# A Strassen-type first GEMM in the second feed-forward layer: seven block products for eight, in five of six token chunks

## The chip, the cores and the metric

The kernel runs on one core of a Trainium2 chip. The metric is the device time of one execution in microseconds (us): the median of 3 runs before the change is 853.1 us (852.42 to 856.21). TensorE (PE) multiplies; each of its matmuls has a weight load of its own (PEld), which the trace records apart. VectorE (DVE), ScalarE (ACT) and GpSimd (POOL) do the element-wise work, SyncE (SP) issues the DMAs.

## What is computed

An mLSTM-like attention over 4 batches x 768 positions, and then two feed-forward layers on its 3072 rows of 320 numbers:

```
x = np.ascontiguousarray(attn_out.transpose(0, 2, 1, 3)).reshape(B * S, H * D)   # (3072, 320)
h = x @ w_in;  g = np.maximum(0.01 * h, h);  x = (g @ w_out)                      # layer 0: 320 -> 2048 -> 320
h = np.maximum(x @ w_in, 0.0);  return (h * h @ w_out).astype(np.float32)         # layer 1: 320 -> 2048 -> 320
```

All in float32. The change is in layer 1, in the product `x @ w_in`.

## The kernel before

Tokens go in 6 chunks of 512 (128 positions of each of the 4 batches), the hidden width of 2048 in 16 tiles of 128 (index j). Full precision comes from splitting each number into a rounded part H and a rest L (both float32r) and adding three products: wH xH + wL xH + wH xL. One tile j of a chunk in layer 1 is:

- `moe_h` (L462 to 486): the contraction over 320 is two blocks of 128 and a rest of 64. Eight matmuls of 512 columns go into one PSUM bank `hp` (L472): three for each of the two blocks, and two for the rest, whose H and L parts lie stacked in one 128-row tile. Then ACT takes the ReLU out of the bank into `g` (L483), DVE squares it (L484), ACT rounds it into `gH` (L485), DVE subtracts into `gL` (L486).
- `out2` (L540 to 563): for each batch three matmuls of 320 columns (L552 to 554) add this tile's share of the second GEMM into one of four banks; after j = 15 the banks are copied out by ACT or DVE (L560, L562) and sent to memory (L563). The four banks rotate over six.

Layer 1's weights arrive during the last chunk of layer 0 and the first of layer 1, and are unpacked by DVE (L432, L434, L437, L448, L443) and ACT (L436, L439), 16 tiles one after the other. `x2_split` (L528) splits a chunk's layer-1 input.

The order of the work on each engine is not written by hand. Every operation is entered with an engine, an estimated length and a key; `Sched.order` (L96) simulates the whole program with these lengths, turns the result round to get new keys (`backward`), repeats that 6 times and then tries 160 random shifts of the keys, and keeps the best plan. Each engine then executes its list strictly in that order. A PSUM bank or an SBUF buffer under a tag is given to its next user when all readers of the last one are done.

Of the kernel before, what the change touches and what calls it, by code (L numbers as in the profile page):

```python
# [8 lines left out]
F32 = mybir.dt.float32  # L9
# [5 lines left out]
ALU = mybir.AluOpType  # L15
# [37 lines left out]
class Sched:  # L53
    SAME = {"PE": 0, "DVE": 130, "ACT": 120, "POOL": 100, "SP": 0}

    def __init__(self):
        self.nodes, self.slots, self.idle = [], {}, []

# [70 lines left out]
    def backward(self, plan, total):  # L129
# [23 lines left out]
    def forward(self):  # L153
# [26 lines left out]
        while done < len(self.nodes):  # L180
# [78 lines left out]
            else:  # L259
# [5 lines left out]
                for m in n.outs:  # L265
                    m.ndep -= 1
                    if m.ndep == 0:
                        t = max(d.end + (self.SAME[m.eng] if d.eng == m.eng else 100) for d in m.deps)
                        heapq.heappush(at, (max(t, now, m.after), 1, m.seq))
# [7 lines left out]
def act(n, psum=False):  # L277
    return (n + (61 if psum else 112)) / 1.2
# [11 lines left out]
def mlstm_moe_kernel(  # L290
# [122 lines left out]
    def weight(layer, j, key):  # L413
# [24 lines left out]
        f32 = lambda: ft().bitcast(F32)  # L438
        op("ACT", act(WR), key, lambda: A.copy(w.t[:, 0:WR], f32()), r=[(fb, fr)], w=[(w, "H"), (w, "C")])  # L439
        c0 = 512 if layer == 0 else 576  # L440
# [22 lines left out]
    def moe_h(layer, c, lo, n, j, key, xk):  # L463
# [9 lines left out]

        op("PE", 8 * mm(n), key, pe, r=[(w, "H"), (w, "L"), (w, "C")] + [(x, k) for k in xk for x in (xH, xL)], w=[(hp, 0)])
        gH, gL = sb("gH", [128, BLK], F32R, 3), sb("gL", [128, BLK], F32R, 3)
# [61 lines left out]

    pools6 = ["attS", "atty", "attm", "acc0", "acc1", "acc2"]

    def out2(c, j, key):  # L540
        w = wt[1, j]
        gH, gL = gs.pop((1, c, 0, j))
        if j == 0:
            acc[1] = [ps(pools6[(4 * c + i) % 6]) for i in range(4)]
        first, last = j == 0, j == NF - 1
        for b in range(B):
            a = acc[1][b]

# [6 lines left out]

            op("PE", 3 * mm(DM), key, pe, r=[(w, "H"), (w, "L"), (gH, 0), (gL, 0)], w=[(a, 0)])
            if last:
                o = sb("aw", [128, DM], slots=3)
                if b % 2 == 0:
# [260 lines left out]
    for layer in range(2):  # L820
        for c in range(NCH):
# [3 lines left out]
            if layer == 1:  # L825
                x2_split(c, base - 20)
            for j in range(NF):
                if layer == 0 and c == 0:
                    continue
                key = base + U * j  # L830
                moe_h(layer, c, 0, BLK, j, key, range(4) if layer == 0 else range(3))
                if layer == 0:
                    out1(c, 0, BLK, j, key + ORDER["outk"] * U)
                else:
                    out2(c, j, key + ORDER["outk"] * U)
            if layer == 0 and c == NCH - 1:
# [69 lines left out]
```

## Time and profile before

| | |
|---|---|
| median of 3 runs | 853.1 us (852.42 to 856.21) |
| the profiled execution, its own time | 856.46 us |
| its span, first to last instruction | 854.7 us |
| PE busy | 836.0 us, 98% of the span, 5161 matmuls recorded |
| DVE busy | 533.6 us (62%) |
| ACT busy | 470.1 us (55%) |
| POOL busy | 97.9 us (11%) |
| TensorE clock granted, mean | 0.991 |

Busy shares are means over stages with different limits: attention with layer 0 reaches to about 510 us, layer 1 fills the rest, 58 us a chunk. A matmul's recorded length includes its way through the array, and matmuls overlap; what one costs in a stream is the distance from its start to the next one's.

### The profile page before, as it was taken

How to read it: one execution, taken by the hardware profiler on the slowest of the kernel's cores; microseconds unless marked ns; L12 is line 12 of the kernel's file. 1: busy time of each engine (PE TensorE's matmuls, PEld its weight loads, DVE VectorE, ACT ScalarE, POOL GpSimd, SP SyncE). 2: the span in 40 equal slices, each digit the busy share in tenths (PEclk: the TensorE clock that was granted, in tenths of full speed). 3: DMA queues.
4: the chain of work that ended last, by engine and by line, in shares of the span. 5: the costliest groups of instructions: out<-in, count | busy, mean ns of one | idle time of the engine just before them, and what ended most of it. 6: DMA issues, size and time to landing. Idle time of an engine off the chain costs nothing.

```text
span 854.7 us, 13738 instructions
## 1 busy us (share of the span) xinstructions
PE 836.0 (98%) x5161; PEld 719.3 (84%) x5166; DVE 533.6 (62%) x974; ACT 470.1 (55%) x933; POOL 97.9 (11%) x134
## 2 busy tenths in 40 slices
PE   9889989999999999999999999999999999999998
PEld 6778878787878877888788889899999999999997
DVE  6799975767676676766657898453443533533433
ACT  8588657757766785676455675343433433433332
POOL 3354731103010210001000000000000000000000
PEclk9799999999999999999999999999999999999999
DMA  7396452435344353552312432000000000000000
GB/s 217 115 324 206 134 162 84 156 100 170 100 153 147 122 158 116 152 160 94 99 69 77 161 136 69 1 32 1 1 31 0 17 15 1 31 1 1 32 1 31
DMA packets 52211, 78.58 MB, mean 92 GB/s; under 512 B 4337, under 2 KB 40785, under 8 KB 52145
## 3 DMA queue, kind: packets, MB, share of 16 engines
q1 hardware_dynamic: 52144, 77.71, 28.5%
q8 instruction: 40, 0.66, 0.3%
q14 instruction: 27, 0.21, 0.1%
HBM read 54.26 MB, written 4.01 MB: 68 GB/s over the span
## 4 chain that ended last, share of the span: by engine, by line
PE 74%; DVE 12%; SPq 4%; ACT 4%; DMA 3%; issue 2%; POOL 0%; DVEq 0%; ACTq 0%; POOLq 0%
PE hp L472 33%; SPq L620 4%; PE acc L503 3%; PE acc L554 3%; PE acc L553 3%; PE acc L552 3%; PE acc L505 3%; PE acc L504 3%; DMA aw<-Adram 2%; PE attS L678 2%; PE acc L508 2%; PE acc L509 2%; ACT aw L669 1%; PE atty L688 1%; DMA T<-X 1%
## 5 line engine op out<-in xcount | busy, mean ns | idle before, releaser
L472 PE MATMUL hp<-xH,w 128*128 128x512 f32 (+1 forms) x995 | 290.1, 388 | 4.9 <-DVE gL L480 3.6
L472 PEld LDWEIGHTS hp<-xH,w 128*128 128x128 f32 x995 | 178.2, 188 | 36.4 <-DVE gL L480 5.0
L472 PE MATMUL hp<-xL,w 128*128 128x512 f32 (+1 forms) x597 | 196.0, 383 | 0.0
L484 DVE TENSOR_TENSOR g<-g 128x512 f32<-128x512 f32 x96 | 66.3, 691 | 119.5 <-ACT g L483 119.5
L472 PEld LDWEIGHTS hp<-xL,w 128*128 128x128 f32 x597 | 111.2, 188 | 23.6
L483 ACT ACTIVATE g<-hp 128x512 f32<-128x512 f32 x96 | 57.3, 597 | 130.3 <-PE hp L472 130.2
L486 DVE TENSOR_TENSOR gL<-g,gH 128x512 fp32r<-128x512 f32 x96 | 66.3, 691 | 56.4 <-ACT gH L485 56.4
L485 ACT CAST gH<-g 128x512 fp32r<-128x512 f32 x96 | 59.6, 620 | 68.9 <-DVE g L484 68.9
L480 DVE TENSOR_TENSOR gL<-hp,gH 128x512 fp32r<-128x512 f32 (+1 forms) x103 | 66.9, 650 | 33.8 <-ACT hp L479 33.0
L478 ACT ACTIVATE gH<-hp 128x512 fp32r<-128x512 f32 (+1 forms) x103 | 58.1, 564 | 46.9 <-PE hp L472 41.8
L503 PE MATMUL acc<-gH,w 128*128 128x512 f32 (+1 forms) x206 | 82.2, 399 | 0.0
L505 PE MATMUL acc<-gL,w 128*128 128x512 f32 (+1 forms) x206 | 77.8, 378 | 0.6 <-DVE gL L480 0.6
L504 PE MATMUL acc<-gH,w 128*128 128x512 f32 (+1 forms) x206 | 77.6, 377 | 0.0
L554 PE MATMUL acc<-w,gL 128*128 128x320 f32 x192 | 59.3, 309 | 0.0
L553 PE MATMUL acc<-w,gH 128*128 128x320 f32 x192 | 59.3, 309 | 0.0
L552 PE MATMUL acc<-w,gH 128*128 128x320 f32 x192 | 59.2, 308 | 0.0
L479 ACT ACTIVATE hp<-hp 128x512 f32<-128x512 f32 (+1 forms) x103 | 57.6, 559 | 0.0
L672 POOL TENSOR_SCALAR_AFFINE_SELECT aw<-aw 128x512 f32<-128x512 f32 x48 | 32.2, 671 | 202.8 <-ACT aw L669 193.0
L669 ACT ACTIVATE aw<-aw,cs 128x128 f32<-128x128 f32 x160 | 50.6, 390 | 7.1 <-DMA aw<-Adram 6.8
L505 PEld LDWEIGHTS acc<-gL,w 128*128 128x128 f32 x206 | 38.7, 188 | 8.4 <-DVE gL L480 0.8
L503 PEld LDWEIGHTS acc<-gH,w 128*128 128x128 f32 x206 | 39.0, 189 | 5.8
L504 PEld LDWEIGHTS acc<-gH,w 128*128 128x128 f32 x206 | 38.9, 189 | 5.6
(165 smaller groups left out, 1447.8 us busy)
## 6 DMA issues: line engine op xcount, KB each, us to landing
T<-X SPq DMA_DIRECT2D x144, 120.0 KB
x<-in_wts_dram SPq DMA_DIRECT2D x16, 704.0 KB
aw<-Adram SPq DMA_DIRECT2D x40, 256.0 KB
nat<-in_nat_dram SPq DMA_DIRECT2D x24, 328.0 KB
qkr<-in_qk_dram SPq DMA_DIRECT2D x16, 360.0 KB
X<-in_wts_dram SPq DMA_DIRECT2D x8, 704.0 KB
T<-in_wts_dram SPq DMA_DIRECT2D x8, 704.0 KB
og<-in_og_dram SPq DMA_DIRECT2D x12, 320.0 KB
```

Source lines behind the costliest of these rows:

```text
L472: T.matmul(hp.t[:, 0:n], w.t[:, col:col + 128], x.t[:, kt, o], start=(s == 0), stop=(s == 7))
L480: op("DVE", dve(n), key, lambda: V.tensor_tensor(out=gL.t[:, 0:n], in0=h(), in1=gH.t[:, 0:n].bitcast(F32), op=ALU.subtract), r=[(hp, 0), ( ...
L484: op("DVE", dve(n), key, lambda: V.tensor_tensor(out=g.t, in0=g.t, in1=g.t, op=ALU.mult), r=[(g, 0)], w=[(g, 0)])
L485: op("ACT", act(n), key, lambda: A.copy(gH.t, g.t), r=[(g, 0)], w=[(gH, 0)])
L486: op("DVE", dve(n), key, lambda: V.tensor_tensor(out=gL.t, in0=g.t, in1=gH.t.bitcast(F32), op=ALU.subtract), r=[(g, 0), (gH, 0)], w=[(gL, 0)])
L503: T.matmul(a[t].t[:, o], w.t[:, hc:hc + 128], gH.t[:, 0:n], start=first, stop=False)
L504: T.matmul(a[t].t[:, o], w.t[:, lc:lc + 128], gH.t[:, 0:n], start=False, stop=False)
L505: T.matmul(a[t].t[:, o], w.t[:, hc:hc + 128], gL.t[:, 0:n], start=False, stop=last)
L552: T.matmul(a.t[:, 0:DM], gH.t[:, s], wH, start=first, stop=False)
L553: T.matmul(a.t[:, 0:DM], gH.t[:, s], wL, start=False, stop=False)
L554: T.matmul(a.t[:, 0:DM], gL.t[:, s], wH, start=False, stop=last)
L669: A.activation(aw.t[:, h], x[:, h], AF.Exp, bias=cs.t[:, 4 * g + h:4 * g + h + 1])
```

## The change

In chunks 1 to 5 of layer 1 two tiles j = 2p and 2p+1 become a pair, and the two 128-row blocks of the contraction times these two tiles are a 2 x 2 block matrix; the 512 tokens are cut into two halves of 256. The 2 x 2 by 2 x 2 block product is formed by Strassen's scheme in Winograd's form: seven block products instead of eight, each of three matmuls (H and L parts) of 256 columns. The rest of 64 rows stays as it was (two matmuls of 256 columns, four times a pair).

- `weight_sums` makes, once for each of the 8 pairs during chunk 0, the sums S1 to S4 of weight blocks on DVE and splits them (S4 in place of block A21, which is no longer needed). They lie in the buffers T, X, qkr, Cst, C32 of earlier stages.
- `x2_sums` replaces `x2_split` for chunks 1 to 5: sums T1 to T4 of the input's blocks, then the same splitting.
- `moe_pair` issues the products into two banks X and Y. Y collects a running sum; ACT copies it out of the bank four times between the products (256 columns each) into buffers `q`. At the end DVE adds q and the bank (L652), takes ReLU and square in one operation (L654), ACT rounds (L655), DVE subtracts (L656).
- `out2` gives its four products of a tile keys of their own (table `OUT`), so that the planner can put them between the block products; the two halves of odd tiles come out swapped and are read so. Its four banks are now fixed; the pairs use two `hp` banks and `acc1`, `acc2` in turn.
- Every product of a pair is entered as a write of its whole bank, so a copy from one half waits for, and holds up, products into the other. From layer 1 on, the planner counts 230 ns from PE to another engine, 250 ns back and 120 ns between the others, where it counted 100.

```
+COPY = 150
+OUT = (1, 2.5, 3, 5, 5.5, 7, 7.3, 7.6)
+    def edge(self, d, m):
+        return 100 if m.seq < self.late else 230 if d.eng == "PE" else 250 if m.eng == "PE" else 120
...
+    def weight_sums(p, key):
...
+        for i, w in enumerate((w0, w1)):
+            op("DVE", dve(256), key, lambda i=i, w=w: V.tensor_tensor(out=a.t[:, i], in0=w.t[:, 0:256].bitcast(F32), in1=w.t[:, 704:960].bitcast(F32), op=ALU.add),
...
+        for o, x, y, f, rd in ((S1, A21, A22, ALU.add, [(a, 1)]), (S2, S1, A11, ALU.subtract, [(s, 0), (a, 0)]),
+                               (S3, A11, A21, ALU.subtract, [(a, 0), (a, 1)]), (S4, A12, S2, ALU.subtract, [(a, 0), (s, 1)])):
...
+        op("ACT", act(3 * CH), key + 0.4, lambda: A.copy(sb_.t[:, at, 0], s3()), r=rd, w=[(sb_, (at, "H"))])
+        op("DVE", dve(3 * CH), key + 0.5, lambda: V.tensor_tensor(out=sb_.t[:, at, 1], in0=s3(), in1=sb_.t[:, at, 0].bitcast(F32), op=ALU.subtract),
...
+    def x2_sums(c, key):
...
+        for k, (o, a, b, rd) in enumerate(((T1, B12, B11, [(x, 0)]), (T2, B22, T1, [(x, 1), (t, 0)]), (T3, B22, B12, [(x, 0), (x, 1)]), (T4, B21, T2, [(x, 1), (t, 1)]))):
+            op("DVE", dve(256), key, lambda o=o, a=a, b=b: V.tensor_tensor(out=o(), in0=a(), in1=b(), op=ALU.subtract), r=rd, w=[(t, k)])
...
+    def moe_pair(c, p, key):
...
+        X, Y = [ps("hp") if p % 2 == 0 else ps(("acc1", "acc2")[i]) for i in range(2)]
...
+        def three(bank, half, a, b, start):
+            o = bank.t[:, 256 * half:256 * half + 256]
+            for i, (u, v) in enumerate(((a[0], b[0]), (a[1], b[0]), (a[0], b[1]))):
+                T.matmul(o, u(), v(), start=start and i == 0, stop=i == 2, skip_group_check=True)
+
+        def two(bank, half, i, w):
+            o = bank.t[:, 256 * half:256 * half + 256]
+            for k in range(2):
+                T.matmul(o, w.t[:, 576:704], xC.t[:, 2 + 2 * k + i], start=False, stop=k == 1, skip_group_check=True)
...
+        prod(Y, 0, A11, B11, 0, start=True)
+        copy(0, 256, 0, (q[0], 0, 0))
+        prod(X, 0, A12, B21, 0.5, start=True, tail=(w0, X, 0, 0))
+        prod(Y, 0, S2, T2, 2)
+        copy(0, 256, 2, (q[1], 1, 0))
+        prod(Y, 1, S3, T3, 3.5)
+        prod(Y, 0, S1, T1, 4)
+        copy(0, 256, 4, (q[1], 0, 1), (q[0], 1, 0))
+        prod(X, 1, S4, B22, 4.5, tail=(w0, X, 1, 1))
+        prod(Y, 1, A22, t4, 6, tail=(w1, Y, 1, 0))
+        op("PE", 2 * mm(256), key + 6.3 * U / 4, lambda: two(Y, 0, 1, w1), r=[(w1, "C"), (xC, 2), (xC, 4)], w=[(Y, 0)])
...
     def out2(c, j, key):
...
-            acc[1] = [ps(pools6[(4 * c + i) % 6]) for i in range(4)]
+            acc[1] = [ps(x) for x in pools4]
...
-            op("PE", 3 * mm(DM), key, pe, r=[(w, "H"), (w, "L"), (gH, 0), (gL, 0)], w=[(a, 0)])
+            op("PE", 3 * mm(DM), key + (OUT[4 * (j % 2) + b] * U / 4 if c else 0), pe, r=[(w, "H"), (w, "L"), (gH, h), (gL, h)], w=[(a, 0)])
...
+                elif j % 2 == 0:
+                    moe_pair(c, j // 2, key)
```

The order that the planner makes of it is the same on PE through all of attention and layer 0 and up to the second tile of layer 1's chunk 0, where the matmuls of one more tile are now drawn ahead of the second GEMM's products. DVE and ACT take the first operations of `x2_sums` and of `weight_sums` already during the last chunk of layer 0. Four places show what moved.

On PE, in the middle of a chunk of layer 1, before: one tile's eight matmuls into an `hp` bank (L472), then twelve for the second GEMM (L552 to 554; `w` is a weight tile, `gH` and `gL` the split hidden tile).

```order
L472 MATMUL hp_6861<-xH_6155,w7_5529 128x512 x4
L472 MATMUL hp_6861<-xL_6162,w7_5529 128x512 x2
L472 MATMUL hp_6861<-xH_6155,w7_5529 128x512
L472 MATMUL hp_6861<-xL_6162,w7_5529 128x512
L552 MATMUL attm_6725<-w5_5450,gH_6831 128x320
L553 MATMUL attm_6725<-w5_5450,gH_6831 128x320
L554 MATMUL attm_6725<-w5_5450,gL_6842 128x320
```

On PE in chunk 1 now, where pair 3 starts (Y is bank `acc2`, X is `acc1`; `X_6051` holds the weight sums S1 to S3 of this pair; L610 is a block product, L615 the rest of 64 rows, L673 to 675 the second GEMM):

```order
L610 MATMUL acc2_6546<-xH_5669,w6_5524 128x256 x2
L610 MATMUL acc2_6546<-xL_5673,w6_5524 128x256
L610 MATMUL acc1_6550<-xH_5669,w6_5524 128x256 x2
L610 MATMUL acc1_6550<-xL_5673,w6_5524 128x256
L615 MATMUL acc1_6550<-x2_0_5190,w6_5524 128x256 x2
L673 MATMUL attS_6438<-w4_5440,gH_6531 128x320
L674 MATMUL attS_6438<-w4_5440,gH_6531 128x320
L675 MATMUL attS_6438<-w4_5440,gL_6544 128x320
L610 MATMUL acc2_6546<-xH_5669,X_6051 128x256 x2
L610 MATMUL acc2_6546<-xL_5673,X_6051 128x256
```

Between the first product into Y and the second, for which Y must have been copied out, now stand the product into X, its rest and one group of the second GEMM.

On PE, still in chunk 1, now: the end of pair 4 in the `hp` banks (the rest into Y, `hp_6612`) and the beginning of pair 6 in the same two banks (`hp_6714` takes the bank that held X, `hp_6720` the one that held Y); before, the next use of a bank stood a whole tile later, as in the rows above.

```order
L673 MATMUL acc0_6456<-w7_5569,gH_6654 128x320
L674 MATMUL acc0_6456<-w7_5569,gH_6654 128x320
L675 MATMUL acc0_6456<-w7_5569,gL_6666 128x320
L615 MATMUL hp_6612<-x2_0_5190,w9_5642 128x256 x2
L610 MATMUL acc2_6650<-xH_5669,qkr_6127 128x256 x2
L610 MATMUL acc2_6650<-xL_5673,qkr_6127 128x256
L610 MATMUL hp_6714<-xH_5669,w12_5799 128x256 x2
L610 MATMUL hp_6714<-xL_5673,w12_5799 128x256
L610 MATMUL hp_6720<-xH_5669,w12_5799 128x256 x2
L610 MATMUL hp_6720<-xL_5673,w12_5799 128x256
```

Six matmuls of 256 columns stand between the last one into Y and the first into the same bank for the pair after next.

On DVE in chunk 0 of layer 1, from the eighth `gL` of that chunk to the tenth, before (the squaring is L484, `gL` is L486):

```order
L486 TENSOR_TENSOR gL_5954<-g_5932,gH_5952 128x512
L484 TENSOR_TENSOR g_5959<-g_5959 128x512
L486 TENSOR_TENSOR gL_5982<-g_5959,gH_5971 128x512
L484 TENSOR_TENSOR g_5987<-g_5987 128x512
L486 TENSOR_TENSOR gL_6010<-g_5987,gH_5999 128x512
```

and now, from the eighth to the ninth and on (squaring L490, `gL` L492, the sums of weight blocks L554 and L561, their lower parts L565 and L568):

```order
L492 TENSOR_TENSOR gL_6005<-g_5974,gH_5999 128x512
L565 TENSOR_TENSOR T_5924<-aw_5966,T_5924 128x384
L561 TENSOR_TENSOR aw_5966<-aw_5473,aw_5966 128x128
L490 TENSOR_TENSOR g_6010<-g_6010 128x512
L568 TENSOR_TENSOR w5_5483<-aw_5966,w5_5483 128x128
L554 TENSOR_TENSOR aw_6028<-w6_5524 128x256
L554 TENSOR_TENSOR aw_6028<-w7_5569 128x256
L492 TENSOR_TENSOR gL_6040<-g_6010,gH_6026 128x512
L561 TENSOR_TENSOR aw_6042<-aw_6028 128x128 x2
L561 TENSOR_TENSOR aw_6042<-aw_6042,aw_6028 128x128
```

Between two `gL` that stood one operation apart, five further ones of 128 to 384 columns now stand; the sums of all eight pairs lie so between the chunk's own operations.

## Rows read from the trace of the kernel before

**Rows 1.** Page of the profile: busy us, share of the span, instructions; granted clock in 40 slices.
```profile
PE 836.0 (98%) x5161; PEld 719.3 (84%) x5166; DVE 533.6 (62%) x974; ACT 470.1 (55%) x933; POOL 97.9 (11%) x134
...
PEclk9799999999999999999999999999999999999999
```
**Rows 2.** Table by stage, layer 1: stretch, length, busy us (count) by engine, clock, DMA share, GB/s.
```profile
core 0: us, PE busy (x) PEld busy (x) DVE busy (x) ACT busy (x) POOL busy (x), PEclk, DMA share, GB/s
560.00:620.00 60.00, 60.00 (x334) 54.21 (x333) 26.35 (x41) 22.61 (x39) 0.00 (x0) 1.00 0.03 12
680.00:740.00 60.00, 60.00 (x336) 54.36 (x336) 25.84 (x39) 22.95 (x40) 0.00 (x0) 1.00 0.04 12
800.00:855.00 55.00, 51.47 (x292) 46.69 (x290) 20.36 (x30) 17.32 (x30) 0.00 (x0) 0.99 0.04 16
```
**Rows 3.** Timeline of PE, layer 1: start us, length us, engine, line, operation, operands.
```profile
563.15 1.09 PE L472 MATMUL hp<-xH,w 128*128 128x512 f32 x4
...
691.06 0.31 PE L552 MATMUL attS<-w,gH 128*128 128x320 f32 x1
...
692.67 0.31 PE L554 MATMUL acc<-w,gL 128*128 128x320 f32 x1
692.81 1.09 PE L472 MATMUL hp<-xH,w 128*128 128x512 f32 x4
```
**Rows 4.** Timeline of PE, layer 0: sixteen matmuls of 256 columns; eight of 512.
```profile
72.08 0.28 PE L503 MATMUL acc<-gH,w 128*128 128x256 f32 x1
...
73.99 0.39 PE L678 MATMUL attS<-X 128*128 128x128 f32 x2
...
500.05 0.39 PE L503 MATMUL acc<-gH,w 128*128 128x512 f32 x1
...
501.87 1.07 PE L472 MATMUL hp<-xH,w 128*128 128x512 f32 x4
```
**Rows 5.** Timeline of PEld in the same stretch of 256 columns.
```profile
72.44 0.19 PEld L504 LDWEIGHTS acc<-gH,w 128*128 128x128 f32 x1
72.56 0.19 PEld L505 LDWEIGHTS acc<-gL,w 128*128 128x128 f32 x1
```
**Rows 6.** Groups by line and shape, ACT and DVE: busy us, mean ns, idle before.
```profile
L479 ACT ACTIVATE hp<-hp 128x256 f32<-128x256 f32 x11 | 4.1, 372 | 0.0
L485 ACT CAST gH<-g 128x512 fp32r<-128x512 f32 x76 | 47.2, 620 | 54.1 <-DVE g L484 54.1
L480 DVE TENSOR_TENSOR gL<-hp,gH 128x256 fp32r<-128x256 f32 x11 | 4.6, 414 | 0.1
L480 DVE TENSOR_TENSOR gL<-hp,gH 128x512 fp32r<-128x512 f32 x4 | 2.7, 684 | 0.0
```
**Rows 7.** Timelines of PE, ACT and DVE where one engine takes over from another.
```profile
579.36 0.30 PE L552 MATMUL acc<-w,gH 128*128 128x320 f32 x1
...
579.62 0.60 ACT L483 ACTIVATE g<-hp 128x512 f32<-128x512 f32 x1 [1.62 <-PE hp L472]
...
580.25 0.69 DVE L484 TENSOR_TENSOR g<-g 128x512 f32<-128x512 f32 x1 [1.52 <-ACT g L483]
...
68.95 0.42 DVE L480 TENSOR_TENSOR gL<-hp,gH 128x256 fp32r<-128x256 f32 x1
...
69.42 0.39 PE L505 MATMUL acc<-gL,w 128*128 128x256 f32 x1 [0.62 <-DVE gL L480]
```
**Rows 8.** Table by stage where layer 1's weights are unpacked (columns as Rows 2).
```profile
456.00:503.00 47.00, 47.00 (x208) 38.54 (x206) 40.60 (x64) 29.44 (x47) 0.00 (x0) 1.00 0.43 146
503.00:533.00 30.00, 30.00 (x160) 26.61 (x159) 28.14 (x45) 18.13 (x30) 0.57 (x1) 1.00 0.25 86
533.00:562.00 29.00, 29.00 (x163) 26.17 (x162) 13.39 (x20) 11.96 (x21) 0.00 (x0) 1.00 0.00 1
```
**Rows 9.** Timelines of DVE and PE at the eighth tile of layer 1's chunk 0.
```profile
533.55 0.69 DVE L486 TENSOR_TENSOR gL<-g,gH 128x512 fp32r<-128x512 f32 x1 [0.69 <-ACT gH L485]
534.16 0.69 DVE L484 TENSOR_TENSOR g<-g 128x512 f32<-128x512 f32 x1
...
536.40 0.30 PE L554 MATMUL attS<-w,gL 128*128 128x320 f32 x1
```

More of the change, by code (lines that the diff above doesn't have):

```diff
@@ L267, in forward @@
                     if m.ndep == 0:
-                        t = max(d.end + (self.SAME[m.eng] if d.eng == m.eng else 100) for d in m.deps)
+                        t = max(d.end + (self.SAME[m.eng] if d.eng == m.eng else self.edge(d, m)) for d in m.deps)
                         heapq.heappush(at, (max(t, now, m.after), 1, m.seq))
@@ L438, in weight @@
         f32 = lambda: ft().bitcast(F32)
-        op("ACT", act(WR), key, lambda: A.copy(w.t[:, 0:WR], f32()), r=[(fb, fr)], w=[(w, "H"), (w, "C")])
+        op("ACT", act(WR), key, lambda: A.copy(w.t[:, 0:WR], f32()), r=[(fb, fr)], w=[(w, "H"), (w, "C"), (w, "A21H")])
         c0 = 512 if layer == 0 else 576
@@ L472, in pe @@
                 T.matmul(hp.t[:, 0:n], w.t[:, col:col + 128], x.t[:, kt, o], start=(s == 0), stop=(s == 7))
-        op("PE", 8 * mm(n), key, pe, r=[(w, "H"), (w, "L"), (w, "C")] + [(x, k) for k in xk for x in (xH, xL)], w=[(hp, 0)])
+        old = [(w, "A21H"), (w, "A21L")] if layer else []
+        op("PE", 8 * mm(n), key, pe, r=[(w, "H"), (w, "L"), (w, "C")] + old + [(x, k) for k in xk for x in (xH, xL)], w=[(hp, 0)])
         gH, gL = sb("gH", [128, BLK], F32R, 3), sb("gL", [128, BLK], F32R, 3)
@@ L543, in out2 @@
         if j == 0:
-            acc[1] = [ps(pools6[(4 * c + i) % 6]) for i in range(4)]
+            acc[1] = [ps(x) for x in pools4]
         first, last = j == 0, j == NF - 1
+        swap = 2 if c and j % 2 else 0
         for b in range(B):
-            a = acc[1][b]
+            a, h = acc[1][b], (b ^ swap) // 2 if c else 0
             def pe(b=b, a=a):
-                s = slice(b * CH, (b + 1) * CH)
+                s = slice((b ^ swap) * CH, ((b ^ swap) + 1) * CH)
                 wH, wL = w.t[:, 256:576], w.t[:, 960:1280]
@@ L820, in mlstm_moe_kernel @@
     for layer in range(2):
+        if layer:
+            sc.late = len(sc.nodes)
         for c in range(NCH):
@@ L824, in mlstm_moe_kernel @@
                 attention(c + 1, [base + ORDER["c0"] + ORDER["cs"] * g for g in range(8)], ORDER["cld"])
-            if layer == 1:
+            if layer == 1 and c == 0:
                 x2_split(c, base - 20)
+            elif layer == 1:
+                x2_sums(c, base - 20)
             for j in range(NF):
@@ L830, in mlstm_moe_kernel @@
                 key = base + U * j
-                moe_h(layer, c, 0, BLK, j, key, range(4) if layer == 0 else range(3))
+                if layer == 0 or c == 0:
+                    moe_h(layer, c, 0, BLK, j, key, range(4) if layer == 0 else range(3))
+                    if layer == 1 and j % 2:
+                        weight_sums(j // 2, key + U)
+                elif j % 2 == 0:
+                    moe_pair(c, j // 2, key)
                 if layer == 0:
```

86 lines of the change are left out of this document (78 added, 8 removed).

## The prediction

> **What bounds the kernel now.** I read the page first: PE is busy 98% of the span, the granted clock is at its full level but for one slice near the start [rows 1]. The table by stage then shows layer 1 apart: PE is busy in all of 560 to 620 and 680 to 740 us, DVE and ACT in under half of them, and only the last stretch has 3.5 us without PE, the end of the program [rows 2]. So layer 1 lasts as long as its stream of matmuls, and what counts is the distance between starts, which the timeline of PE shows. DVE and ACT matter where PE comes to wait for them, and where they are dense: the unpacking of layer 1's weights, DVE busy 28.1 of 30 us [rows 8].
>
> **The products.** From 563.15 to 692.81 us lie 36 tiles: 3.60 us each, 7.20 a pair [rows 3]. The twelve matmuls of the second GEMM take 691.06 to 692.81, 1.75 us, 0.146 each. The eight of 512 columns are left with 1.85 us, 0.231 each. A pair has 16 of these, 3.70 us. Afterwards it has seven products of three matmuls and four rests of two, 29 of 256 columns. Their distance stands in layer 0: sixteen from 72.08 to 73.99, 0.119 each; eight of 512 there took 1.82 us, 0.2275 each [rows 4]. Layer 1's 512 are 1.6% slower than layer 0's for a reason that no row tells; if 256 suffer it too they take 0.121. So 29 cost 3.46 to 3.52 us; I take 0.120, 3.48. The 24 matmuls of the second GEMM stay. Gain 0.216 us a pair (0.18 to 0.23), over 5 chunks of 8 pairs 8.6 us (7.2 to 9.3). It is under an eighth of the first GEMM because the rest of 64 rows is not saved and two 256 cost a little more than one 512.
>
> A weight load is recorded with 0.19 us, longer than the distance of 0.119, and yet loads start 0.12 apart, so they run under the matmuls and under one another [rows 5]. The Trainium skill, "TensorE: Matmul & The Clock Gate", section "The mechanism", says that a weight load overlaps matmuls in flight only when it goes to other rows of the array; by that rule this change, which nearly doubles the loads of the first GEMM, would be far slower (rival D), and the trace does not bear it out. The same page, section "Back-to-back issue gap", gives N/2.4 + 2.5 ns for a single matmul, 109 ns for 256 columns and 216 for 512; by it the gain would be 0.29 us a pair, 11.5 in all (an estimate), but both measured distances are longer.
>
> **The copies out of Y.** Each pair makes PE wait for ACT three times: before the second and the third product into Y for one copy, before the last for two. The price if nothing hid it: the last 512 columns are in at 579.36, ACT starts at 579.62, so 0.26 us; the copy of 256 columns 0.37 [rows 6, 7]; back to PE, DVE ends at 69.37, the matmul starts at 69.42 and is 0.11 us longer than its like (0.39 for 0.28), so 0.16 [rows 4, 7]. That is 0.79 us for one copy and 1.16 for two, 2.7 a pair, 110 us in all, against a gain of 8.6. What hides it is the work that the order puts between. I counted it in all 40 pairs, 0.12 and 0.146 a matmul: the least is 0.96 us before the second product, 0.96 before the third, and 1.56 before the last, apart from 0.88 in the very last pair. So as long as ACT takes a copy at once, 0.3 us is lost in all. If every copy stood behind a rounding of 512 columns, 0.62 us [rows 6], the short places would add up to 1.2 + 1.2 + 1.8 = 4.2 us. ACT has about 4 x 0.37 + 2 x 0.62 = 2.7 us of work in a pair of 7.0, so mostly it is free: I take 0.3.
>
> **Handing the banks back.** A bank goes to the next pair when DVE has added it: 0.26 + 0.68 + 0.16 = 1.10 us after its last matmul [rows 6, 7]. Counted in the order, Y's `hp` bank is wanted back after 0.72 us twice (the place shown in the order) and after 1.3 or more else; `acc2` six times after 1.2 to 1.32, else after 1.56 or more; the banks of X after at least 2.7. That costs 2 x 0.38 = 0.8 us if the add starts at once. DVE takes a queue in order: with one operation of 0.6 us, from start to start [rows 9], ahead of each add it is 5.6 us, with two 17.5. In DVE's list the add of Y mostly follows the add and square of X, which are ready a product or more earlier, and DVE's six operations of a pair are 3.6 us of 7.0. I take 1.0.
>
> **The second GEMM's waits.** From the last matmul into a bank to a usable `gL` it is 0.26 + 0.68 + 0.69 + 0.62 + 0.69 + 0.16 = 3.1 us. The order leaves at least 4.2 us everywhere but at the end of the program. There the last two operations are split in halves: 0.26 + 0.41 + 0.41 + 0.37 + 0.41 + 0.16 = 2.0, with another half's operation of 0.4 between, 2.4 to 2.8; PE has five groups of the second GEMM to do, 2.2 us, and two more matmuls that need only `gH`. That is 0 to 0.6 us, with the short copy 0 to 1.2; I take 0.5 for the end together. The fixed output banks are wanted again 3.2 us after a chunk's last use, a copy-out needs about 1.1: nothing.
>
> **The sums, in chunk 0.** DVE gets 66 more instructions between the second weight tile's unpacking and the sixteenth `gL` of layer 1: 16 sums of 256, 32 of 128, 8 subtractions of 384 and 8 of 128, 12 operations of the x2 sums, less 6 of `x2_split` and 4 that go to POOL. At 0.61 us start to start for 512 [rows 9], and by the 0.27 that 256 columns fewer save [rows 6] about 0.34 for 256, 0.25 for 128 and 0.47 for 384, they come to 20 us. From 456 to 562 us DVE was busy 82 of 106 us [rows 8], so they fit, but tightly. The tight part is up to the eighth `gL`: 6.5 us of the 20 stand before it, and DVE had 8.3 us idle in 456 to 533. What lateness PE bears: that `gL` was ready at 534.24 and wanted at 536.40, 2.1 us [rows 9], and the new order gives the second GEMM 1.8 us more by drawing one tile's products ahead. If none of the 6.5 us falls into idle time, PE waits 2.6 us; if a third does, nothing. I take 0.5. After the eighth, DVE needs 25 us for eight tiles that take PE 29. In the later chunks the x2 sums add about 3 us of DVE a chunk, where it is half free: nothing.
>
> **The sum.** -8.6 for the products, +1.0 for the banks, +0.5 for the end (the 0.3 of the last copy in it), +0.5 for chunk 0: -6.6 us. The profiled execution took 856.46 and would take 849.9; it lies 3.4 above the median, which I forecast with: 853.1 - 6.6 = 846.5 us. About 0.5%, 4.3 us, is what a measurement of this kernel can tell from no change: faster means below 848.8, slower above 857.4.
>
> **Rivals.**
> A, the forecast: 844 to 848.8, the unknown terms between nothing and half of their bounds. Chance 0.69.
> B, small waits eat half: the copies behind ACT's rounding (4.2), one operation before each add (5.6) or chunk 0 (2.6) come near their upper ends, any two of them; gain 0 to 4.3, about 850.5. For it: DVE's density [rows 8] and queues in strict order. Against: the plan was made with 0.23 and 0.25 us for the ways that the rows show as 0.26 and 0.16, and with longer operations than these, so the places mostly have room. Chance 0.19.
> C, the other side, DVE's queue at the hand-back: the add of Y sits behind a subtraction into `gL` that itself waits for ACT. PE loses the sum of what each of the 38 re-uses lacks; by the counted distances the gain is gone at a mean lateness of 0.72 us and it is slower by 0.5% from 0.95; at two operations (1.2 us) it gives 853.1 - 8.6 + 17.5 + 1.0 = 863. Against it: DVE 3.6 of 7.0 us busy. Chance 0.04.
> D, weight loads come to bind: 256 columns stream in 0.2275 - 0.119 = 0.108 us; with 0.19 for the load [rows 5] on top, 29 x 0.298 = 8.6 us a pair instead of 3.70, 40 x 4.9 = 196 us more, 1049. Against: sixteen such matmuls in a row at 0.119 [rows 4]. Chance 0.01.
> E, all waits vanish and 256 columns run at half of 512 or at the issue gap: gain 9.3 to 11.5, 841.6 to 843.8. For it: every counted distance but a few is above its need. Chance 0.07.
>
> So faster 0.76 (A and E), same 0.19, slower 0.05. Range 844.0 to 850.5: the likeliest case and half of B; its own range is 844 to 848.8.
>
> **What would show it.** Layer 1's PE stays without gaps but for some of 0.1 to 0.4 us before products into `hp` and `acc2`; the 256-column matmuls start 0.119 to 0.121 apart; a chunk of layer 1 lasts 55.9 to 56.1 us where it lasted 57.6; layer 0 ends where it did. DVE is about 95% busy from 456 to 560 and some 55 to 60% after, ACT 40 to 45%. B would show as PE waiting for DVE's `gL` around 515 to 540 us, or as many waits of several tenths in each chunk; C as PE waiting for L652 of about a microsecond each in every pair. A distance of 0.127 us between 256-column matmuls (3.70 / 29) would take the whole gain and prove the first step wrong, and so would another order of time in layer 0, where nothing on PE has moved.

## The result and the profile after

In four runs each the changed kernel took 843.8 us in the median (842.6 to 846.1) and the kernel before 854.3: a ratio of 0.988 [0.984, 0.992]. Five further rounds gave 844.3 against 853.0, 0.990 [0.987, 0.992]. The forecast was 846.5 in a range from 844.0; the first median lies 0.2 below the range and the second just inside. The profiled execution of the changed kernel took 846.1, its span 844.4. Of twenty executions of the kernel before beside the further rounds, the two with a mean granted clock of 0.991 and 0.992 took 856.6 and 855.6, the others 850.2 to 854.9; two of the first round's four took 856.2 and 855.6, but their clock is not on record.

The page after (busy us, share, instructions; then the clock in 40 slices), to set beside [rows 1]:

```profile
PE 823.8 (98%) x5681; PEld 733.1 (87%) x5686; DVE 607.6 (72%) x1150; ACT 483.3 (57%) x1041; POOL 113.0 (13%) x138
...
PEclk9999999999999999999999999999999999999999
```

PE issues 520 matmuls more and is busy 12 us less, still 98% of the span. The clock line has lost the slice at 7. That is no work of the change, which moves nothing on PE there; the table of 10 us stretches shows what it was. Before:

```profile
10.00:20.00 10.00, 10.00 (x74) 9.22 (x73) 6.71 (x11) 8.80 (x22) 4.11 (x5) 0.87 0.85 250
20.00:30.00 10.00, 9.78 (x41) 8.44 (x43) 5.37 (x12) 4.58 (x13) 3.68 (x5) 0.50 0.55 166
```

After, same columns as [rows 2]:

```profile
20.00:30.00 10.00, 7.51 (x78) 6.08 (x81) 9.78 (x18) 6.52 (x18) 7.03 (x8) 1.00 0.55 178
...
503.00:533.00 30.00, 29.65 (x160) 26.09 (x159) 29.25 (x51) 20.18 (x35) 5.58 (x5) 1.00 0.23 81
533.00:562.00 29.00, 29.00 (x170) 26.54 (x169) 27.18 (x70) 15.97 (x36) 7.52 (x1) 1.00 0.00 1
562.00:620.00 58.00, 57.94 (x445) 57.74 (x444) 36.41 (x58) 24.21 (x59) 0.00 (x0) 1.00 0.04 13
...
680.00:740.00 60.00, 60.00 (x457) 60.00 (x456) 36.80 (x60) 24.11 (x59) 0.00 (x0) 1.00 0.05 15
```

In the one profile of before TensorE ran at 0.50 from 20 to 30 us, half of its full level, and did 41 matmuls where the other did 78. So the first 500 us can't be compared between the two profiles. What can is the stretch of layer 1, from the first matmul of its second GEMM to the program's last matmul, PE's order being the same up to its beginning, and what comes behind it: 3.58 us before, 3.57 after. The timeline of PE before:

```profile
510.93 0.30 PE L552 MATMUL attS<-w,gH 128*128 128x320 f32 x1
...
851.16 0.31 PE L554 MATMUL acc<-w,gL 128*128 128x320 f32 x1
```

And after:

```profile
508.52 0.30 PE L673 MATMUL attS<-w,gH 128*128 128x320 f32 x1
...
567.86 0.40 PE L610 MATMUL hp<-xH,w 128*128 128x256 f32 x2
568.10 0.28 PE L610 MATMUL hp<-xL,w 128*128 128x256 f32 x1
568.22 0.40 PE L615 MATMUL hp<-x,w 128*128 128x256 f32 x2
568.45 0.40 PE L610 MATMUL hp<-xH,T 128*128 128x256 f32 x2
568.69 0.28 PE L610 MATMUL hp<-xL,T 128*128 128x256 f32 x1
568.80 0.31 PE L673 MATMUL attS<-w,gH 128*128 128x320 f32 x1
...
840.79 0.31 PE L675 MATMUL atty<-w,gL 128*128 128x320 f32 x1
```

340.23 us became 332.28 (the last start is at 840.795 before rounding to the row): 7.95 us, all of it in layer 1. Before it the two profiles differ by a further 2.41 us. Eight matmuls of 256 columns start within 0.94 us, 0.118 each. This stretch repeats to 0.05 us from run to run (332.28 and 332.24 for the changed kernel, 340.23 before and once more in a run below), where the whole time scatters by 2 or 3; it is the measure used in the experiments.

Summed over all starts in the stretch: before, 744 matmuls of 512 columns took 171.83 us, 231.0 ns each, and 1151 of 320 columns 168.40, 146.3 each. After, 104 of 512 took 24.23, 1160 of 256 took 138.38, and the 1151 of 320 took 169.67. So the first GEMM of chunks 1 to 5, waits included, gives 640 x 0.2310 - 138.38 = 9.45 us, and 1.5 are lost elsewhere.

Where PE starts late is seen at few places. The list of PE's waits in the stretch has one line:

```profile
PE attS L675 <- DVE gL L492: 0.4, 1, 0.4
```

It is the eighth tile of chunk 0. On the timeline PE wants at 530.56, 0.15 after its last start, what DVE writes until 531.01:

```profile
530.33 0.68 DVE L492 TENSOR_TENSOR gL<-g,gH 128x512 fp32r<-128x512 f32 x1
...
530.41 0.31 PE L674 MATMUL attS<-w,gH 128*128 128x320 f32 x1
...
531.07 0.41 PE L675 MATMUL attS<-w,gL 128*128 128x320 f32 x1 [0.35 <-DVE gL L492]
```

The start is 0.51 us late and the matmul 0.10 longer. Waits under some 0.3 us don't appear as such, since the recorded end of a matmul covers them (0.28 us recorded for 256 columns, the next start after 0.12); they are read from distances between starts. One such place is in chunk 0, where PE takes an `hp` bank back from ACT, whose ReLU ends at 512.13:

```profile
511.53 0.60 ACT L489 ACTIVATE g<-hp 128x512 f32<-128x512 f32 x1
...
511.88 0.39 PE L477 MATMUL hp<-xL,w 128*128 128x512 f32 x1
512.18 0.50 PE L477 MATMUL hp<-xH,w 128*128 128x512 f32 x1
```

The start at 512.18 is 0.07 us late, and the matmul is 0.11 longer than its like. The two tight hand-backs of `hp` to the pair after next look like this:

```profile
593.98 0.40 PE L615 MATMUL hp<-x,w 128*128 128x256 f32 x2
...
594.42 0.69 DVE L652 TENSOR_TENSOR g<-nat,hp 128x512 f32<-128x512 f32 x1 [0.93 <-PE hp L615]
...
594.82 0.28 PE L610 MATMUL hp<-xL,w 128*128 128x256 f32 x1
595.16 0.50 PE L610 MATMUL hp<-xH,w 128*128 128x256 f32 x2
595.50 0.28 PE L610 MATMUL hp<-xL,w 128*128 128x256 f32 x1
```

From 594.82 to 595.16 it is 0.34 where 0.12 is usual, and the next two take 0.34 where they usually take 0.24: 0.32 us, until the addition at 594.42 has handed the bank back at 595.11. The other, at 636.89, costs 0.33.

### The profile page after: what moved, and what is told of

Read it like the earlier page. It is cut to its first block, busy times and chain, and to the rows that moved or that the text cites. A ratio compares the mean times of both kernels' runs of the same rounds, so it can differ in the third digit from the quotient of the medians.

```text
span 844.4 us, 15024 instructions
## 1 busy us (share of the span) xinstructions
PE 823.8 (98%) x5681; PEld 733.1 (87%) x5686; DVE 607.6 (72%) x1150; ACT 483.3 (57%) x1041; POOL 113.0 (13%) x138
## 4 chain that ended last, share of the span: by engine, by line
PE 66%; DVE 14%; ACT 6%; DMA 5%; issue 5%; SPq 3%; POOL 1%; DVEq 0%; ACTq 0%; POOLq 0%
PE hp L477 13%; PE hp L610 6%; PE acc L610 6%; PE acc L509 3%; PE acc L511 3%; PE acc L510 3%; DMA aw<-Adram 3%; SPq L741 3%; PE hp L615 2%; PE acc L615 2%; ACT aw L790 2%; PE attS L675 2%; PE attm L675 2%; PE acc L673 2%; PE atty L675 2%
## 5 line engine op out<-in xcount | busy, mean ns | idle before, releaser
L477 PE MATMUL hp<-xH,w 128*128 128x512 f32 (+1 forms) x595 | 171.8, 386 | 4.9 <-DVE gL L486 3.6
L477 PEld LDWEIGHTS hp<-xH,w 128*128 128x128 f32 x595 | 106.8, 189 | 25.9 <-DVE gL L486 5.0
L477 PE MATMUL hp<-xL,w 128*128 128x512 f32 (+1 forms) x357 | 115.5, 379 | 0.0
L486 DVE TENSOR_TENSOR gL<-hp,gH 128x512 fp32r<-128x512 f32 (+1 forms) x103 | 67.0, 650 | 33.3 <-ACT hp L485 32.6
L484 ACT ACTIVATE gH<-hp 128x512 fp32r<-128x512 f32 (+1 forms) x103 | 58.1, 564 | 44.6 <-PE hp L477 38.1
L509 PE MATMUL acc<-gH,w 128*128 128x512 f32 (+1 forms) x206 | 82.6, 401 | 0.0
L511 PE MATMUL acc<-gL,w 128*128 128x512 f32 (+1 forms) x206 | 78.2, 380 | 0.6 <-DVE gL L486 0.6
L510 PE MATMUL acc<-gH,w 128*128 128x512 f32 (+1 forms) x206 | 78.0, 379 | 0.0
L477 PEld LDWEIGHTS hp<-xL,w 128*128 128x128 f32 x357 | 66.5, 189 | 13.2
L655 ACT CAST gH<-g 128x512 fp32r<-128x512 f32 (+1 forms) x82 | 50.2, 613 | 43.1 <-DVE g L654 43.1
L656 DVE TENSOR_TENSOR gL<-g,gH 128x512 fp32r<-128x512 f32 (+1 forms) x82 | 55.3, 675 | 20.3 <-ACT gH L655 19.7
L793 POOL TENSOR_SCALAR_AFFINE_SELECT aw<-aw 128x512 f32<-128x512 f32 x48 | 32.6, 680 | 200.7 <-ACT aw L790 199.4
L654 DVE SCALAR_TENSOR_TENSOR g<-g 128x512 f32<-128x512 f32 (+1 forms) x82 | 55.3, 675 | 1.2
L631 ACT COPY nat<-hp 128x256 f32<-128x256 f32 x40 | 15.0, 375 | 47.4 <-PE hp L610 47.3
L514 PE MATMUL acc<-gH,w 128*128 128x512 f32 (+1 forms) x103 | 40.4, 392 | 0.0
L515 PE MATMUL acc<-gL,w 128*128 128x512 f32 (+1 forms) x103 | 38.7, 376 | 0.0
L631 ACT COPY nat<-acc 128x256 f32<-128x256 f32 x40 | 14.9, 372 | 41.5 <-PE acc L610 41.0
```

What stands on the lines that cost most here:

```text
L477: T.matmul(hp.t[:, 0:n], w.t[:, col:col + 128], x.t[:, kt, o], start=(s == 0), stop=(s == 7))
L484: op("ACT", act(n, True), key, lambda: A.activation(gH.t[:, 0:n], h(), AF.Prelu, alpha=0.01), r=[(hp, 0)], w=[(gH, 0)])
L486: op("DVE", dve(n), key, lambda: V.tensor_tensor(out=gL.t[:, 0:n], in0=h(), in1=gH.t[:, 0:n].bitcast(F32), op=ALU.subtract), r=[(hp, 0), ( ...
L509: T.matmul(a[t].t[:, o], w.t[:, hc:hc + 128], gH.t[:, 0:n], start=first, stop=False)
L510: T.matmul(a[t].t[:, o], w.t[:, lc:lc + 128], gH.t[:, 0:n], start=False, stop=False)
L511: T.matmul(a[t].t[:, o], w.t[:, hc:hc + 128], gL.t[:, 0:n], start=False, stop=last)
```

## The experiments

Theory 1: the change is worth what its matmuls save by their start distance, less what the few places lack by which the order of PE falls short of a hand-over. The rivals are named in each expectation. Below, "the stretch" is that of layer 1 defined above, 332.24 us in the changed kernel (340.23 before).

**The changed kernel once more.** No edit; on the chip and beside the runs of the next three.

> The changed kernel itself, timed again. Theory 1 (the products alone): layer 1 is 8.0 us shorter, 9.5 from 40 pairs at 29 x 0.1193 instead of 16 x 0.231 us, less 1.5 of waits and slower matmuls; everything before layer 1 is unchanged, so the difference to the kernel before is 7.5 to 8.5 us. Rival 1 (something else gives 2 us of the 10.3 between the medians, in attention, layer 0 or the buffers that moved): 9.5 to 10.5 us, and the first product of layer 1's second GEMM starts 2 us earlier at an equal granted clock.

844.33 us, ratio 0.990 [0.987, 0.992]: 9.0 us less than before by the ratio, 8.7 by the medians, between the two expectations, the interval of 6.8 to 11.1 holding both. The stretch, 8.0 us shorter, speaks for theory 1, and the next run decides.

**The new plan without the products.**
```
...
-                elif j % 2 == 0:
-                    moe_pair(c, j // 2, key)
+                moe_h(layer, c, 0, BLK, j, key, range(4) if layer == 0 else range(3))
...
```
`x2_split` in all chunks, no sums, and the second GEMM's entries as before; the planner's costs, fixed output banks and moved buffers stay.

> Without the pairs: all six chunks of layer 1 go through moe_h and x2_split again, the second GEMM's products have the keys of before; the planner's new waiting costs, the four fixed output banks, the moved buffers stay. Theory 1: as long as the kernel before, within 1 us. Rival 1: 2 us faster than before, since what gives the rest is still in it.

852.69 us, 0.999 [0.998, 1.001], the stretch 340.23, to the hundredth that of before. The rest of the change shows no gain (by the interval it is worth at most 1.7 us): the rival falls, and the pairs are worth 852.7 - 844.3 = 8.4 us by the medians, 8.0 by the stretch.

**Pairs in the last two chunks only.**
```
+FIRST = 4
...
-                if layer == 0 or c == 0:
+                if layer == 0 or c < FIRST:
...
```
and the same condition in `out2` and for `x2_sums`; the sums of weights then stand in chunk 3.

> Pairs in chunks 4 and 5 alone, the weight sums in chunk 3, where DVE is half free. Theory 1: two fifths of 9.5, so 3.8 us faster than before, less 0.3 to 0.6 for the end and for copies; no wait for gL around 530 us. Rival 1: 5.5 us faster, since 2 us do not depend on the pairs. If the sums in the dense chunk 0 cost more than they show, it would keep more than two fifths of the change's gain.

849.82 us, 0.996 [0.994, 0.997]: 3.2 us less than before, the stretch 337.06, also 3.2 less. Two fifths of the 7.95 of five chunks are 3.2: the gain goes by the chunk.

**An eighth product in each pair** (one block product is added a second time, so the output is another).
```
         prod(X, 0, A12, B21, 0.5, start=True, tail=(w0, X, 0, 0))
+        prod(X, 0, A12, B21, 1)
```

> Each pair gets one more block product of three matmuls, the product into X a second time (so that share is counted twice in the output), with no new wait. Theory 1, PE without slack: 40 x 3 x 0.1193 = 14.3 us slower than the changed kernel, 6 us slower than before. Rival 2 (the pairs are paced by copies and hand-backs, PE has room that no gap shows): less than 10 us slower than the changed kernel.

859.34 us, 1.007 [1.004, 1.009]: +15.0 against the changed kernel, +14.2 in the stretch, where 40 x 3 x 0.119 is 14.3. A product costs its matmuls in full; nothing of it is hidden, and nothing but matmuls is in it.

**The planner's old costs.**
```
-        return 100 if m.seq < self.late else 230 if d.eng == "PE" else 250 if m.eng == "PE" else 120
+        return 100
```
with `COPY = 0` and the factors of 1.4 in `moe_pair` gone.

> The planner's costs go back to what they were (100 ns for a hand-over from engine to engine everywhere, nothing for a wait counted by bank, vector and activation lengths not stretched by 1.4); the products, the spread second GEMM and the waits stay. Theory 1: a wait costs what the order of PE fails to put between, so counting gives the price. In this order the twelve matmuls of cover before the second product into Y hold 0.59 us in the median where one copy needs 0.79, short by 5.9 us over the 40 pairs, 0.8 before the third, 0.1 before the last, and none of the hand-backs is short: 6.8 us more than the changed kernel, about -2 to -3 us against the kernel before; if ACT is also 0.3 us late at each copy, some 24 us more. PE would be seen to wait for ACT's copies before the second product of most pairs, 0.1 to 0.2 us each. Rival 3: the engines run far enough ahead that where the order puts the work doesn't matter: within 1 us of the changed kernel, -8 to -10 against before.

850.68 us, 0.998 [0.996, 1.000]: 6.4 worse than the changed kernel (medians of two sets), 5.2 in the stretch. A typical place, PE and ACT:

```profile
642.14 0.28 PE L610 MATMUL hp<-xL,w 128*128 128x256 f32 x1
...
642.15 0.37 ACT L631 COPY wl<-hp 128x256 f32<-128x256 f32 x1 [0.60 <-PE hp L610]
...
642.26 0.40 PE L615 MATMUL hp<-x,w 128*128 128x256 f32 x2
...
642.58 0.50 PE L610 MATMUL hp<-xH,X 128*128 128x256 f32 x2
```

The two matmuls from 642.26 end their turn at 642.50; the next product into that bank waits for the copy, which ends at 642.52, and starts 0.08 late and 0.1 slow. 34 of the 40 pairs have such a place, each with a late start and a slow one behind it, 6.6 us together. All late starts of the stretch come to 6.9 us, where they are 1.6 in the changed kernel; the difference agrees with the 5.2. The expectation had put 6.8 on top of the changed kernel and so left out the 1.1 that the same count gives there. So the planner's hand-over costs are worth some 5 us: at the old costs over half the gain is gone. Rival 3 falls.

**The second GEMM as one block.**
```
...
-            op("PE", 3 * mm(DM), key + (OUT[4 * (j % 2) + b] * U / 4 if c else 0), pe, r=[(w, "H"), (w, "L"), (gH, h), (gL, h)], w=[(a, 0)])
...
+        op("PE", 12 * mm(DM), key + (OUT[4 * (j % 2)] * U / 4 if c else 0), pe, r=[(w, "H"), (w, "L")] + [(x, h) for x in (gH, gL) for h in hs_], w=[(a, 0) for a in accs])
```

> The second GEMM's twelve matmuls of a tile are entered in the plan as one operation, not spread as four groups of three. Theory 1: the spreading itself earns nothing; what counts is that enough stands between a product and its next use of Y. In this order the short places add up to 0.7 us before the products and 1.5 us at the hand-backs, 2.2 in all where the changed kernel has 1.1 by the same count: +1 us against it, -8 against before; up to +7 if the adds are 0.6 us late. Rival 4: without the spreading the copies out of Y stand in the way of PE as worked out in the prediction (0.79 us each unhidden): +5 us or more against the changed kernel.

844.75 us, 0.991 [0.989, 0.993], the stretch 332.98: 0.7 more than the changed kernel, 1 expected. By the count in the expectation the planner finds other cover in this order, which lacks 2.2 us in all where the changed kernel's lacks 1.1; the spreading by itself is worth under a microsecond, and rival 4 falls.

**No sums of weights** (blocks of the weights stand in for them; the output is another).
```
...
-        ws = lambda k: (lambda: sb_.t[:, at, 0, k * CH:(k + 1) * CH], lambda: sb_.t[:, at, 1, k * CH:(k + 1) * CH], [(sb_, (at, "H")), (sb_, (at, "L"))])
+        ws = lambda k: wb((w0, w1)[k % 2], 1)
...
-                        weight_sums(j // 2, key + U)
```

> The sums of layer 1's weight blocks are not formed; blocks of the weights themselves stand in as operands of the products (the output is another one). Chunk 0 of layer 1 has 48 vector operations fewer, everything else stays. Theory 1: the sums cost only the one wait of PE for the eighth gL at 530.4 us (0.35 idle, 0.5 in all) and perhaps a little speed of the 320-column matmuls: 0.4 to 0.8 us less than the changed kernel, -9 to -10 against before. Rival 5: the dense vector work of chunk 0 holds PE up in ways not seen as waits: 2 us or more less, -11 or beyond.

843.25 us, 0.989 [0.987, 0.991]; the stretch 331.68, 0.6 less. DVE has 14.9 us of work from 533 to 562 instead of 27.2, and of PE's late starts only those of chunk 0 are gone: the wait for `gL`, 0.6, and the place at 512.18, 0.2; the 256-column matmuls took 0.2 more. Rival 5 falls.

**One more vector operation ahead of each addition.**
```
+    def added(g, x, bank, o):
+        q = x.t.rearrange("p k n -> p (k n)")[:, o]
+        for _ in range(1):
+            V.tensor_tensor(out=g.t[:, o], in0=q, in1=q, op=ALU.add)
+        V.tensor_tensor(out=g.t[:, o], in0=q, in1=bank.t[:, o], op=ALU.add)
...
```
`added` stands in place of the addition of L652, at X and at Y.

> Each addition of a block of X to a block of Y on the vector engine is preceded by one more operation of the same width whose result is overwritten; the orders of all engines stay as in the changed kernel. The bank of Y is handed back about 0.61 us later at every one of its re-uses. Theory 1: the counted distances give 5.9 us of waiting at the hand-backs where it was 0.8, so +5.2 us against the changed kernel, -4 against before, with PE waiting for these additions in place of standing still nowhere; DVE then is busy some 70% of a pair and delays nothing else. Rival C of the prediction: DVE's queue is what binds, its lateness adds up from operation to operation, and the gain is gone: +9 us or more against the changed kernel. Rival 6: the distances have slack that counting misses: less than +2 us.

848.09 us, 0.995 [0.993, 0.997]: +3.8 by the medians, +5.0 in the stretch, 5.2 expected. PE's waits there:

```profile
PE hp L616 <- DVE g L598: 1.4, 3, 0.6
PE attm L681 <- DVE gL L662: 0.5, 1, 0.5
PE acc L616 <- DVE g L598: 0.4, 1, 0.4
PE attS L681 <- DVE gL L492: 0.4, 1, 0.4
```

The rest is in starts that are late without a recorded wait. The counted distances hold here; rival C, 9 us or more, and rival 6, under 2, don't.

**Two more ahead of each addition**: `range(2)` in the same place.

> As the run with one more vector operation ahead of each addition, but with two of them: the banks of Y and X are handed back about 1.22 us later than in the changed kernel, orders unchanged. Theory 1 (a hand-back costs what its counted distance lacks): 18.3 us of waiting where it was 0.8, so +17.5 us against the changed kernel, about +9 against before; the run with one gave +4.8 by its median, so the step from one to two should be over twice that from none to one. It is the case that the prediction's rival C prices at 863. Rival 7 (vector operations cost in proportion to their number, by the engine's load): another +5, about 853, level with before.

897.77 us, 1.052 [1.048, 1.055]: +53 against the changed kernel, three times theory 1's price and ten times rival 7's. PE's waits:

```profile
PE acc L616 <- DVE g L598: 16.4, 14, 2.2
PE hp L616 <- DVE g L598: 15.4, 12, 2.1
PE attS L681 <- DVE gL L662: 6.1, 11, 0.8
```

The waits stand where rival C had put them, at the hand-backs, for both `hp` and `acc`, up to 2.2 us each. Late starts at the hand-backs make some 39 us of the 54.5 by which the stretch is longer. Counting with a fixed lateness of 1.22 us fails here; the last run below takes up why.

**Each copy out of Y three times.**
```
- ... lambda o=o, i=i, h=h: A.copy(o.t[:, i], Y.t[:, 256 * h:256 * h + 256]) ...
+ ... lambda o=o, i=i, h=h: [A.copy(o.t[:, i], Y.t[:, 256 * h:256 * h + 256]) for _ in range(3)] ...
```

> Each copy out of a bank of Y is done three times into the same place; the orders of all engines stay as in the changed kernel. A bank of Y comes free 0.74 us later before the second and third product, 1.48 us later before the last, which waits for two copies. Theory 1: by the counted distances PE lacks 2.0, 1.9 and 19.3 us over the 40 pairs, 23.2 in all where it was 0.3: +23 us against the changed kernel, about 867, with PE waiting for the copies before the last product into Y in most pairs, about 0.5 us each. ACT then has some 5.7 us of work in a pair of 7, and its queue may add to it. Rival 6 (slack that counting misses): under +10. Rival 8 (the counted cover is no cover, each copy's time falls on PE): 160 copies of 0.74 us, +118.

876.50 us, 1.028 [1.025, 1.030]: +32, in the stretch +32.6. One of the last copies, ACT and PE:

```profile
640.88 1.18 ACT L631 COPY nat<-hp 128x256 f32<-128x256 f32 x3 [0.64 <-PE hp L610]
...
641.96 1.19 ACT L631 COPY wl<-hp 128x256 f32<-128x256 f32 x3
...
642.44 0.31 PE L675 MATMUL attm<-w,gL 128*128 128x320 f32 x1
...
643.20 0.62 PE L610 MATMUL hp<-x,w 128*128 128x256 f32 x3 [0.45 <-ACT wl L631]
```

The place is the predicted one (the last product into Y, for two copies): with the slow starts behind them the late ones there make 24.1 us where 19.3 were counted; those at the second and third product make 7.3 for 3.9. The price is 1.4 times the count. ACT is busy 44.6 of the 60 us from 680 to 740; whether its queue gives the rest wasn't tried. Rivals 6 and 8 fall: of 118 us of added copies the order hides nearly three quarters.

**Each subtraction into `gL` three times.**
```
- ... V.tensor_tensor(out=gL.t[:, o], in0=g.t[:, o], in1=gH.t[:, o].bitcast(F32), op=ALU.subtract) ...
+ ... [V.tensor_tensor(out=gL.t[:, o], in0=g.t[:, o], in1=gH.t[:, o].bitcast(F32), op=ALU.subtract) for _ in range(3)] ...
```

> The run with two more vector operations ahead of each addition cost 53 us against the changed kernel where the counted distances gave 17.5. Here the same number of operations goes to the other end of the chain: each subtraction into gL is done three times, so the load of DVE is that of the earlier run, about 6.5 of 7 us a pair, but the addition that hands a bank back has no longer way of its own. Theory 9 (place: what lies between a product and the hand-back of its bank costs, and the lateness goes round from hand-back to product to copy to addition): gL comes 1.2 us later, 4.3 us after the bank's last matmul where the order leaves at least 4.2, and the additions stand behind one longer operation at times: +2 to +15 us against the changed kernel. Theory 10 (load: a vector engine that is some 90% busy holds PE up wherever its operations stand): +40 us or more.

891.37 us, 1.045 [1.042, 1.048]: +47, in the stretch +46.4. PE's waits:

```profile
PE attS L675 <- DVE gL L656: 24.4, 49, 1.6
PE attm L675 <- DVE gL L656: 1.1, 2, 1.0
```

Theory 9's price falls: DVE holds PE up wherever the operations stand, at `gL` this time and hardly at a bank. Theory 10 is borne out in number. But its words, a DVE some 90% busy, don't say when: in the changed kernel DVE is busy 29.25 of 30 us from 503 to 533 and 27.18 of 29 behind it, a larger share than in either run, and PE loses 0.8 us there. The table of chunk 3, from the first matmul of its second GEMM to that of the next chunk, tells more (columns as [rows 2]; the changed kernel, one more operation, two more, the subtraction three times):

```profile
680.02:735.48 55.46, 55.46 (x423) 55.46 (x422) 34.95 (x56) 22.62 (x56) 0.00 (x0) 1.00 0.04 13
...
680.07:735.53 55.46, 55.46 (x424) 55.46 (x423) 45.80 (x75) 23.09 (x56) 0.00 (x0) 1.00 0.04 14
...
705.94:769.13 63.19, 57.43 (x424) 55.68 (x422) 56.01 (x89) 23.59 (x55) 0.00 (x0) 1.00 0.03 11
...
696.06:760.03 63.97, 59.48 (x423) 55.48 (x422) 57.04 (x91) 23.81 (x55) 0.00 (x0) 1.00 0.04 12
```

The chunk's matmuls need 55.46 us. With 45.80 us of work on DVE the chunk is as long as ever; with 56.01 and 57.04 DVE has about as much work in it as PE (recorded lengths overlap a little; at the closest starts that these runs show it is an estimated 53 to 55.5 us), so there is hardly time left in which one of the two could wait for the other. That rival, DVE as a second bound, the expectation of the two added operations lacks. It doesn't give the whole price: the chunk grows by 7.7 and 8.5 us, and DVE itself stands idle for 7 in each. Which waits of the two engines for each other make these up, these runs don't separate, and the run with the longer busy time on DVE costs less in all (46 against 54, some 3 of the 54 being the clock, see the end).

## Why the prediction was right

**The bound.** That layer 1 lasts as long as PE's starts is shown: an added product costs 14.2 of 14.3 us, while 12 us less of DVE work in chunk 0 give 0.6.

**The products** were the term that was mis-sized: 8.6 us forecast, with 9.3 as its upper end, 10.1 measured. Without the 0.65 of the two hand-backs the 1160 matmuls took 137.7 us, 118.7 ns each, so the gain is 147.8 - 137.7 = 10.1. I had taken 0.120, in case what makes layer 1's 512 columns 1.6% slower than layer 0's reached the 256 too; it did not. A nanosecond and a third, 1160 times, is the 1.5 us that the forecast of the products was low. The 1.6% itself was read from eight matmuls of layer 0: the 218 of 512 columns from 460 to 510 us start 228.7 ns apart in the mean, so the difference is 1.0%.

The Trainium skill, "TensorE: Matmul & The Clock Gate", section "The mechanism", says that a weight load overlaps matmuls in flight only when it goes to other rows of the array, though the same section also lets a load into a background weight buffer go ahead. By the first of these alone the loads would have stood on PE's path (rival D). The rows are against it: from 680 to 740 us PEld is busy 60.00 of 60.00 and PE loses nothing.

**The copies out of Y**: nothing to see in the changed kernel but 0.10 us at the very end. That it is the order which hides them is shown by the old costs (+5) and the tripled copies (+32).

**Handing the banks back**: 1.0 forecast, 0.65 measured, at the two `hp` places that had been counted; the additions started at once. **Chunk 0**: 0.5 forecast, 0.6 measured, at the eighth `gL` as named. (The working there says that PE waits for nothing if a third of the 6.5 us falls into idle time; by its own terms, 2.1 + 1.8 us borne, it takes two fifths.) **The end**: 0.5 forecast, 0.2 measured. Some 0.7 more stood nowhere in the forecast: 0.2 is the hand-over from ACT at 512.18, the rest is spread over the 320-column matmuls (147.4 ns in the mean, waits included, for 146.3), and no row gives it a place. Together: -10.1 + 0.65 + 0.6 + 0.2 + 0.7 = -7.95. The losses came to 2.15 where 2.0 were forecast, and that is in part luck: the banks and the end were put 0.65 too high together, which about covers the 0.7. So of the difference between 6.6 forecast and 8.0 measured in layer 1 nearly all is the products' 1.5.

**The rivals.** B (small waits) would have shown in many starts; ten were over 25 ns late. C does not happen here, but its mechanism exists: with two more operations ahead of each addition the waits stand where it put them, and the time is 898, not the 863 that its count gave. E's gain of 9.3 to 11.5 holds what the products gave, but the waits did not vanish, and its price isn't what was measured: 256 columns at half of layer 1's 512 would start 115.5 ns apart, which is a gain of 13.9 us and not in E's own range; the 118.7 measured is close to the 119 that the forecast read in layer 0.

**The rest of the medians' gain**, 8.7 to 10.6 us against 8.0 in layer 1, is within the scatter: the intervals, 7.3 to 13.3 us in the first measurement and 6.8 to 11.1 in the second, both hold 8.0. In the profiles it lies before layer 1's second GEMM, which begins at 505.3 to 508.5 us in those of the changed kernel and the experiments, and at 510.93 in that of before, with its clock at half around 20 to 30 us. It begins at 506.80 in the changed kernel timed again and at 506.59 without the pairs. No step of the change accounts for the rest, and the run without pairs has none of it.

Close to the forecast were also: a chunk of 55.8 us (four from 568.80 to 791.98; 55.9 to 56.1 forecast), DVE busy 92% from 456 to 562 (about 95 forecast) and 62% from there to 800 (55 to 60), ACT at 40% (40 to 45). That layer 1's second GEMM began 2.4 us earlier would by the prediction's last sentence have spoken against its first step; PE's matmuls are the same up to there, so it is the clock of the one profile and scatter.

## What to carry to other kernels

On a bound engine, price added or saved instructions by the distance between starts of their own shape, read over more than a few of them, and put no penalty on it that another shape shows: here that penalty was 1.5 us of a gain of 10. Count, for every hand-over, what the order puts between: that gave the losses of the changed order, and of one more vector operation, to a few tenths. But count also the work of the engine off the path in a stage against the time that the bound engine needs for it. With DVE busy for 46 us in a chunk of 55 the count held; with 56 and 57 the whole loss was 54 and 46 us, and for the first of these the count had given 17.5; with each copy on ACT done three times it gave 23 of 33. And look for a stretch inside the program that repeats from run to run: here it resolved 0.1 us where the whole time scatters by 2 or 3.

## What was not expected of the hardware

TensorE's clock fell in the run with two more operations ahead. PE had stood still for 2.2 us (640.04 to 642.20); the table of that stretch:

```profile
638.00:640.00 2.00, 2.00 (x16) 1.83 (x14) 2.00 (x5) 0.57 (x2) 0.00 (x0) 1.00 0.00 0
640.00:642.20 2.20, 0.04 (x1) 0.00 (x0) 1.71 (x4) 1.14 (x4) 0.00 (x0) 1.00 0.02 4
642.20:645.70 3.50, 3.50 (x18) 3.50 (x19) 2.69 (x5) 0.99 (x2) 0.00 (x0) 0.64 0.00 0
645.70:646.30 0.60, 0.60 (x4) 0.60 (x4) 0.00 (x0) 0.00 (x0) 0.00 (x0) 0.50 0.00 0
646.30:650.80 4.50, 4.50 (x35) 4.50 (x34) 2.55 (x4) 0.65 (x2) 0.00 (x0) 0.96 0.01 4
```

The granted clock went to half (0.50 from 645.70 to 646.30, so 1.2 of 2.4 GHz) after work had come back, and from 643.28 to 646.59 matmuls of 320 columns started 0.267 us apart instead of 0.147. It happened at two places of the stretch, behind the longest and the third longest delay of a start (2.3 and 2.0 us), and cost some 3 us of the 54 (1.6 each by the distances between starts); behind a start that came 2.2 us late at 599.66, and behind others 1.5 to 1.8 us late, the clock stayed at full level. And a PEld that is busy all the time is no bound: 0.19 us are recorded for each load, while loads start 0.12 apart.
